# Seven quarter products for the second product of a fused attention and MLP kernel

## The chip, the cores and the metric

One core of one Trainium2 chip. The metric is the device time of one execution in microseconds (us), as the median of several executions. The trace of one execution gives start and duration of every instruction on TensorE (PE; its weight loads PEld), VectorE (DVE), ScalarE (ACT), GpSimd (POOL) and of the DMA queues.

Ratios below are the mean time of one kernel's fast runs over that of the other's of the same rounds on the same chip, so they are not quite the ratio of the medians that are quoted. A run is set aside as slow when it is over 1.5% above the fastest of its kernel.

## The reference

```python
B, H, S, D = 8, 8, 576, 64          # attention: 4 heads with a sliding window of 32,
scores = q @ k.T / sqrt(D)          # 4 heads with every 4th key of the last 128
attn = softmax(where(mask, scores, -1e9)) @ v
x = attn.transpose(0, 2, 1, 3).reshape(4608, 512)
h = x @ w_in                        # 512 -> 2048
g = maximum(h, 0) ** 2
out = g @ w_out                     # 2048 -> 512
```

## The kernel before

The 4608 tokens are cut into nine chunks of 512. For chunk c, the first product gives `ph` (16 tiles of 128 hidden units by 512 tokens), ACT applies relu, DVE squares into `g`; the second product gives four tiles `po` of 128 tokens by 512 outputs. Python generators hand out this work in half-steps (`yield`), and the attention of batch b takes `pump(n)` half-steps of chunk b-1 between its own blocks. So the order on every engine is fixed when the program is built.

```python
def mm1_gen(c, g):
    xs = xT[:, :, c * TOKC : (c + 1) * TOKC]
    for ffc in range(NFF):                                  # 16 steps
        ph = pmool.tile([P, TOKC], FP32, ..., tag="pm")     # 4 PSUM banks in turn
        for dmk in range(NDM):                              # 4 matmuls of 512 columns
            nc.tensor.matmul(ph, wi[...], xs[:, dmk, :], ...)
            if dmk == 1:
                yield
        rt = osb.tile([P, TOKC], FP16, ..., tag="rt")
        nc.scalar.activation(rt, ph[:], ACTF.Relu)
        nc.vector.tensor_mul(g[:, ffc, :], rt, rt)
        yield

def mm2_gen(c, g):
    for t in range(TOKC // P):
        po = pmool.tile([P, DM], FP32, ..., tag="pm")
        for ffc in range(NFF):
            mm2(c, g, po, t, ffc)                           # 16 matmuls of 512 columns
            if ffc % 2 == 1 and ffc < NFF - 1:
                yield
        store(c, t, po)                                     # ACT copy, then a store
        yield

for b in range(2, B):
    pending.append(moe_gen(b - 1))
    ...
    pump(16 if b == 2 else 4)
    attn_scores(b, 4)              # four blocks: matmuls, exp on ACT, mask on DVE
    ...
    attn_values(b, lambda: pump(2 if b == 2 else 3))
    pump(1000)
```

`attn_values` issues the matmuls `pav_0`, `pav_1`, `pav_2` (sliding heads; DVE normalises each into an `x_p` by a reciprocal and a multiplication), the transposes `px_0`, which need the first two `x_p`, then four blocks `paw` with `px_1` and the transposes `py` among them. Score blocks, `pav` and `paw` share two PSUM buffers.

The softmax here doesn't subtract the row's maximum and nothing guards it: scores larger than these inputs give would overflow.

## Time and profile before

| what | value |
|---|---|
| time | 327.25 us, median of 4 (326.17 to 328.54) |
| span of the profiled execution | 327.1 us |
| PE, DVE, ACT busy | 94%, 50%, 51% |
| chunk with attention beside it (chunks 2 to 6) | 32.35 us |
| chunk without (7 and 8) | 27.62 us |
| granted PE clock | 0.984 |

The busy shares are averages over the span. The chain of work that ended last tells which engine sets the pace where: here PE from 80 us to the end. The lines are shown in the prediction.

### The profile page before, as it was taken

To read this page: it belongs to the slowest core of one execution; us is meant where nothing else is said; L and a number is where in the kernel's file an instruction comes from. 1 tells how busy PE (TensorE), PEld (TensorE's weight loads), DVE (VectorE), ACT (ScalarE), POOL (GpSimd) and SP (SyncE) were. 2 spreads that over 40 slices of the span, in tenths; PEclk is the share of its full clock that TensorE was granted. 3 is DMA by queue.
4 is the path that set the end of the run, shared out by engine and by line. 5 is a ranking of instruction groups with operands and counts; after the bars stand their busy time and mean duration, and the time that the engine had idled before them with its cause. 6 is when DMAs were issued, how large, how long until landed. Compare 5 with 4: busy or idle time off the path is not lost.

```text
span 327.1 us, 6310 instructions
## 1 busy us (share of the span) xinstructions
PE 307.9 (94%) x2492; PEld 156.3 (48%) x2492; DVE 162.5 (50%) x348; ACT 168.3 (51%) x300; POOL 81.5 (25%) x139
## 2 busy tenths in 40 slices
PE   5869879996999999999999999999999999999995
PEld 2764344542455455445544554455445544444442
DVE  4584694535662795079408840884098404303500
ACT  2845591264822972397239723972396237415611
POOL 4460660261301800190019001900140010000000
PEclk9999996998999999999999999999999999999999
DMA  8999999989999879589948993899200010021011
GB/s 185 231 194 244 205 183 205 226 171 196 232 205 202 166 171 257 92 178 199 168 142 177 207 197 104 180 207 213 87 34 3 32 66 32 0 95 37 0 64 64
DMA packets 83181, 47.85 MB, mean 146 GB/s; under 512 B 68048, under 2 KB 79056, under 8 KB 82768
## 3 DMA queue, kind: packets, MB, share of 16 engines
q1 hardware_dynamic: 74708, 26.12, 41.5%
q0 software_dynamic: 7072, 19.80, 27.6%
q10 hardware_dynamic: 1372, 1.54, 1.7%
q8 instruction: 19, 0.31, 0.4%
q14 instruction: 10, 0.08, 0.1%
HBM read 39.85 MB, written 16.52 MB: 172 GB/s over the span
## 4 chain that ended last, share of the span: by engine, by line
PE 78%; DMA 12%; ACT 4%; DVE 2%; POOL 1%; issue 1%; SPq 1%; POOLq 0%
PE po L270 35%; PE ph L255 33%; DMA sq<-in_k_dram 6%; DMA QKTx<-dk 3%; DMA dk<-in_k_dram 3%; PE paw L474 2%; PE pav L460 2%; ACT QKTd L143 2%; PE pz L428 1%; PE ps L409 1%; ACT AT L381 1%; PE px L489 1%; PE py L507 1%; DVE AT L382 1%; POOL nq L145 1%
## 5 line engine op out<-in xcount | busy, mean ns | idle before, releaser
L270 PE MATMUL po<-wo,g 128*128 128x512 f16 x576 | 137.7, 384 | 0.0
L255 PE MATMUL ph<-xT,wi 128*128 128x512 f16 x576 | 136.1, 382 | 0.3 <-ACT xT L513 0.3
L266 DVE TENSOR_TENSOR g<-rt 128x512 f16<-128x512 f16 x144 | 76.6, 547 | 105.4 <-ACT rt L265 104.8
L265 ACT ACTIVATE rt<-ph 128x512 f16<-128x512 f32 x144 | 83.8, 604 | 28.5 <-PE ph L255 24.0
L255 PEld LDWEIGHTS <-wi 128*128 128x128 f16 x576 | 52.8, 98 | 58.3 <-issue 1.9
L270 PEld LDWEIGHTS <-g 128*128 128x128 f16 x576 | 53.0, 99 | 55.8 <-issue 2.2
L288 ACT COPY ot<-po 128x512 f32<-128x512 f32 x35 | 20.5, 587 | 72.2 <-PE po L270 72.2
L289 POOL DMA_DIRECT2D out_dram<-ot x28 | 15.5, 553 | 147.9 <-ACT ot L288 147.9
L495 ACT COPY xT<-px 128x576 f16<-128x576 f16 x16 | 10.2, 637 | 25.7 <-PE px L489 25.7
L382 DVE TENSOR_TENSOR AT<-AT,maskp 128x576 f16<-128x576 f16 x32 | 19.6, 636 | 7.6 <-ACT AT L381 7.1
L145 POOL CAST vd<-sd 128x512 f16<-128x512 f32 x32 | 22.9, 754 | 0.0
L443 DVE TENSOR_TENSOR x_d<-paw,rcp_d 72x512 f16<-72x512 f32 x32 | 22.0, 687 | 1.1
L381 ACT ACTIVATE AT<-ps 128x576 f16<-128x576 f32 x32 | 19.2, 657 | 3.7 <-PE ps L409 3.1
L381 ACT ACTIVATE AT<-pz 128x576 f16<-128x576 f32 x32 | 19.2, 669 | 0.3
L161 POOL CAST vp<-sv 128x512 f16<-128x512 f32 x24 | 16.2, 709 | 5.1 <-DMA sv<-in_v_dram 5.1
L442 DVE RECIPROCAL rcp_d<-paw 72x8 f32<-72x8 f32 x32 | 6.5, 202 | 21.9 <-PE paw L474 21.8
L443 DVE TENSOR_TENSOR x_p<-pav,rcp_p 96x512 f16<-96x512 f32 x24 | 16.5, 687 | 0.8
L513 ACT COPY xT<-py 128x576 f16<-128x576 f16 x16 | 10.3, 641 | 11.8 <-PE py L507 11.8
L382 DVE TENSOR_TENSOR AT<-AT,maskd 128x576 f16<-128x576 f16 x32 | 14.9, 495 | 2.4 <-ACT AT L381 2.0
L327 PE MATMUL pj<-zz 128*128 128x128 f16 (+1 forms) x124 | 14.5, 252 | 1.2 <-DVE zz L208 1.2
L474 PEld LDWEIGHTS <-AT 128*128 128x128 f16 x256 | 12.2, 98 | 7.0 <-issue 0.4
L474 PE MATMUL paw<-vd,AT 128*128 128x65 f16 x256 | 13.3, 193 | 0.3 <-DVE rcp_d L442 0.3
(64 smaller groups left out, 144.8 us busy)
## 6 DMA issues: line engine op xcount, KB each, us to landing
out_dram<-ot POOLq DMA_DIRECT2D x28, 256.0 KB, 2.4
sv<-in_v_dram SPq DMA_DIRECT2D x40, 128.0 KB, 7.5
sd<-in_v_dram SPq DMA_DIRECT2D x7, 512.0 KB, 6.3
dk<-in_k_dram POOLq DMA_DIRECT2D x12, 288.0 KB, 6.5
dk<-in_q_dram POOLq DMA_DIRECT2D x12, 288.0 KB, 7.7
wi<-in_moe_w_in_dram POOLq DMA_DIRECT2D x2, 1024.0 KB, 10.6
wo<-in_moe_w_out_dram POOLq DMA_DIRECT2D x4, 512.0 KB, 11.4
sd<-in_v_dram SPq DMA_DIRECT2D x7, 288.0 KB
```

The lines of the kernel that those rows point to most:

```text
L145: eng.tensor_copy(o, i)
L161: nc.gpsimd.tensor_copy(vp[:, m : m + 2, :, 0:D], sv[:, m : m + 2, :, :])
L255: nc.tensor.matmul(ph, wi[:, dmk, ffc * P : ffc * P + P], xs[:, dmk, :], start=(dmk == 0), stop=(dmk == NDM - 1),)
L265: nc.scalar.activation(rt, ph[:], ACTF.Relu)
L266: nc.vector.tensor_mul(g[:, ffc, :], rt, rt)
L270: nc.tensor.matmul(po, g[:, ffc, t * P : (t + 1) * P], wo[:, ffc, :], start=(ffc == 0), stop=(ffc == NFF - 1),)
L288: nc.scalar.copy(ot, po)
L289: (nc.gpsimd if c < B - 1 else nc.sync).dma_start(out=rows, in_=ot)
L381: nc.scalar.activation(AT[:, u, 0:UW], ps[:, :, 0 : UW // 2], ACTF.Exp, scale=scale)
L382: nc.vector.tensor_mul(AT[:, u, 0:UW], AT[:, u, 0:UW], mask)
L443: nc.vector.tensor_tensor(out=x[0:w], in0=pv[:, :, :, 0:D], in1=rcp[0:w].unsqueeze(3).to_broadcast([w, 2, HH, D]), op=ALU.mult,)
L474: nc.tensor.matmul(pav[:, e, h * (D + 2) : h * (D + 2) + D + 1], AT[:, 4 + h, off : off + P], vd[:, t, 2 * a + e, h, 0 : D + 1], start=Tru ...
```

## The change

The idea is Strassen's (in Winograd's form): cut `g` and `w_out` into quarters, and get the product from seven products of quarters instead of eight. It asks for four sums of quarters of `w_out` (made once), four sums of quarters of `g` (for every chunk, on DVE), and for sums of the results, made partly by accumulating in PSUM and partly by DVE. Matmuls have 256 columns instead of 512, and there are 112 instead of 64 of them. Chunk 0 keeps the old product. To make room on DVE, squares now go in pairs of 1024 columns (the last pair singly) and four of the eight pairs move to ACT. To make room in memory, `g` has one buffer instead of two; the trace shows no wait for it at a chunk's start (in chunk 4 ACT's first square starts at 182.28, 0.03 us after the relu that it needs). The attention is spread differently over the half-steps. Core of the diff, cut:

```diff
+    def hidden_sums(g, sm, i0, i1):
+        ...
+        nc.vector.tensor_add(s1, a21, a22)
+        nc.vector.tensor_sub(s2, s1, a11)
+        nc.vector.tensor_sub(s3, a11, a21)
+        nc.vector.tensor_sub(s4, a12, s2)
+
+    BY_ACT = (0, 2, 4, 5)
+    SUMS_AT = {7: (0, 3), 13: (3, 6), 14: (6, 7), 15: (7, 8)}
+
+    def relu_squared(c, ffc, g, ph, rts):
+        ...
+        nc.scalar.activation(rt[:, o, :], ph[:], ACTF.Relu)
+        if i == NK - 1:
+            nc.vector.tensor_mul(g[:, ffc, :], rt[:, o, :], rt[:, o, :])
+        elif o == 1 and i in BY_ACT:
+            nc.scalar.activation(g[:, ffc - 1 : ffc + 1, :], rt, ACTF.Square)
+        elif o == 1:
+            nc.vector.tensor_mul(g[:, ffc - 1 : ffc + 1, :], rt, rt)
...
-            rt = osb.tile([P, TOKC], FP16, name=f"rt{c}_{ffc}", tag="rt")
-            nc.scalar.activation(rt, ph[:], ACTF.Relu)
-            nc.vector.tensor_mul(g[:, ffc, :], rt, rt)
+            relu_squared(c, ffc, g, ph, rts)
+            if sm is not None and ffc in SUMS_AT:
+                hidden_sums(g, sm, *SUMS_AT[ffc])
             yield
...
+        a = bank("poa")
+        yield from product(a, gv[:, :, 0, 0:HT], B11, True)
+        s1 = part("s1")
+        nc.scalar.copy(s1, a)
+        yield
+        b_ = bank("pob")
+        yield from product(b_, sm[:, 1], T[:, 1], True)
+        u2 = part("u2")
+        nc.vector.tensor_add(u2, b_, s1)
+        yield
+        yield from product(a, gv[:, :, 1, 0:HT], B21, False)
+        nc.scalar.copy(otu[:, :, 0:HM], a)
+        ...                             # four more products into b_ and c_, four more additions
...
-        pump(16 if b == 2 else 4)
+        if b == 2:
+            for _ in weight_sums():
+                pump(2)
+            pump(4)
+        else:
+            pump(13)
...
-        attn_values(b, lambda: pump(2 if b == 2 else 3))
+        attn_values(b, lambda: pump(2))
```

In the texts "square 14" is the square of step 14, "sums of pair 6" those of steps 12 and 13, and so on.

More of the change, by code (lines that the diff above doesn't have):

```diff
@@ L57 @@
     stg = ctx.enter_context(tc.tile_pool(name="stg", bufs=1))
-    natp = ctx.enter_context(tc.tile_pool(name="natp", bufs=2))
     xp = ctx.enter_context(tc.tile_pool(name="xp", bufs=4))
-    gp = ctx.enter_context(tc.tile_pool(name="gp", bufs=2))
+    gp = ctx.enter_context(tc.tile_pool(name="gp", bufs=1))
+    tp = ctx.enter_context(tc.tile_pool(name="tp", bufs=1))
     osb = ctx.enter_context(tc.tile_pool(name="osb", bufs=4))
+    otp = ctx.enter_context(tc.tile_pool(name="otp", bufs=3))
     papool = ctx.enter_context(tc.tile_pool(name="papool", bufs=2, space=bass.MemoryType.PSUM))
@@ L83 @@
     sd = stg.tile([P, 2, HH, DIL * D], FP32, name="sd")
-    sq = stg.tile([QB, 2, HH, 6 * D], FP32, name="sq")
+    sq = gp.tile([QB, 2, HH, 6 * D], FP32, name="sq", tag="sm")
+    early = tp.tile([QB, 2, 2, 12 * D * 2], FP16, name="early", tag="T")
+    nq_ = early[:, 0].rearrange("p i (j h d) -> p i j h d", j=6, h=HH)
+    nd_ = early[:, 1].rearrange("p i (g x) -> p i g x", g=2)
     ident = const.tile([P, P], FP16, name="ident")
@@ L113, in load_v, with load_dilated_qk @@
         load_dilated_v(b, nc.sync)
-    def dilated_buffer(b):
-        return natp.tile([QB, 2, 2, 12 * D], FP16, name=f"nd{b}", tag="nd")
-    def load_dilated_qk(b, nd):
+    def load_dilated_qk(b):
         for i, src in ((1, k), (0, q)):
@@ L121, in load_dilated_qk @@
             for e in range(2):
-                nc.gpsimd.dma_start(out=nd[48 * e : 48 * (e + 1), i, :, :], in_=s4[e])
+                nc.gpsimd.dma_start(out=nd_[48 * e : 48 * (e + 1), i, :, :], in_=s4[e])
     def load_w_in():
@@ L147, in cast_sliding_qk @@
     def cast_sliding_qk(b, engs):
-        n = natp.tile([QB, 2, 6, HH, D], FP16, name=f"nq{b}", tag="nq")
         for i in (1, 0):
@@ L153, in cast_sliding_qk @@
                     engs[2 * i + half],
-                    n[:, i, j0 : j0 + 3, :, :],
+                    nq_[:, i, j0 : j0 + 3, :, :],
                     sq[:, i, :, D * j0 : D * (j0 + 3)].rearrange("p h (j d) -> p j h d", d=D),
                 )
-        return n
     def cast_sliding_v(m0=0, m1=NB):
@@ L211 @@
     nc.scalar.activation(warm, warm, ACTF.Exp)
-    nds = {0: dilated_buffer(0)}
-    load_dilated_qk(0, nds[0])
+    load_dilated_qk(0)
     make_identity(nc, ident)
@@ L247, with weight_sums, mm1_gen @@
     )
-    def mm1_gen(c, g):
+    HT = TOKC // 2
+    HM = DM // 2
+    NK = NFF // 2
+    g_of = lambda g: g.rearrange("p (i o) t -> p i o t", o=2)
+    wo_of = wo.rearrange("p (i o) m -> p i o m", o=2)
+    wsum = {}
+    B11, B12 = wo_of[:, :, 0, 0:HM], wo_of[:, :, 0, HM:DM]
+    B21, B22 = wo_of[:, :, 1, 0:HM], wo_of[:, :, 1, HM:DM]
+    def weight_sums():
+        T = wsum["T"] = tp.tile([P, 4, NK, HM], FP16, name="T", tag="T")
+        for i, x, y in (
+            (0, B12, B11),
+            (1, B22, T[:, 0]),
+            (2, B22, B12),
+            (3, B21, T[:, 1]),
+        ):
+            for k0 in range(0, NK, 4):
+                ks = slice(k0, k0 + 4)
+                nc.vector.tensor_sub(T[:, i, ks, :], x[:, ks, :], y[:, ks, :])
+                yield
+    def hidden_sums(g, sm, i0, i1):
+        v = g_of(g)[:, i0:i1]
+        a11, a12 = v[:, :, 0, 0:HT], v[:, :, 1, 0:HT]
+        a21, a22 = v[:, :, 0, HT:TOKC], v[:, :, 1, HT:TOKC]
+        s1, s2, s3, s4 = (sm[:, i, i0:i1, :] for i in range(4))
+        nc.vector.tensor_add(s1, a21, a22)
[5 more added lines that the diff above has]
+    def relu_squared(c, ffc, g, ph, rts):
+        i, o = divmod(ffc, 2)
+        if o == 0:
+            rts[i] = osb.tile([P, 2, TOKC], FP16, name=f"rt{c}_{i}", tag="rt")
+        rt = rts[i]
+        nc.scalar.activation(rt[:, o, :], ph[:], ACTF.Relu)
[5 more added lines that the diff above has]
+            nc.vector.tensor_mul(g[:, ffc - 1 : ffc + 1, :], rt, rt)
+    def mm1_gen(c, g, sm=None):
         xs = xT[:, :, c * TOKC : (c + 1) * TOKC]
+        rts = {}
         for ffc in range(NFF):
@@ L276, in mm2 @@
         )
-    def store(c, t, po):
-        ot = osb.tile([P, DM], FP32, name=f"ot{c}_{t}", tag="ot")
-        rows = out[(c * 4 + t) * P : (c * 4 + t + 1) * P, :]
-        if (c, t) == (NTOKC - 1, 3):
-            h = DM // 2
-            nc.scalar.copy(ot[:, 0:h], po[:, 0:h])
-            nc.sync.dma_start(out=rows[:, 0:h], in_=ot[:, 0:h])
-            nc.vector.tensor_copy(ot[:, h:], po[:, h:])
-            nc.scalar.dma_start(out=rows[:, h:], in_=ot[:, h:])
-            return
-        nc.scalar.copy(ot, po)
-        (nc.gpsimd if c < B - 1 else nc.sync).dma_start(out=rows, in_=ot)
@@ L291, in mm2_gen, with store @@
-    def mm2_gen(c, g):
-        for t in range(TOKC // P):
-            po = pmool.tile([P, DM], FP32, name=f"po{c}_{t}", tag="pm")
-            for ffc in range(NFF):
-                mm2(c, g, po, t, ffc)
-                if ffc % 2 == 1 and ffc < NFF - 1:
-                    yield
-            store(c, t, po)
-            yield
+    def store(c, t, po, ots):
+        if t % 2 == 0:
+            ots[t // 2] = otp.tile([P, 2, DM], FP32, name=f"ot{c}_{t}", tag="ot2")
+        ot = ots[t // 2]
+        nc.scalar.copy(ot[:, t % 2, :], po)
+        if t % 2 == 1:
+            rows = out[(c * 4 + t - 1) * P : (c * 4 + t + 1) * P, :]
+            nc.gpsimd.dma_start(out=rows.rearrange("(t p) m -> p t m", p=P), in_=ot)
@@ new lines, in mm2_strassen_gen, with bank, product, part @@
+    def mm2_strassen_gen(c, g, sm):
+        gv = g_of(g)
+        T = wsum["T"]
+        def bank(name):
+            return pmool.tile([P, 2, HM], FP32, name=f"{name}{c}", tag="pm")
+        def product(acc, lhs, rhs, first):
+            for t in range(2):
+                for k in range(NK):
+                    nc.tensor.matmul(
+                        acc[:, t, :],
+                        lhs[:, k, t * P : (t + 1) * P],
+                        rhs[:, k, :],
+                        start=(first and t == 0 and k == 0),
+                        stop=(k == NK - 1),
+                        skip_group_check=True,
+                    )
+                    if k % 4 == 3 and (t, k) != (1, NK - 1):
+                        yield
+        def part(name):
+            return osb.tile([P, 2, HM], FP32, name=f"{name}{c}", tag="u", bufs=3)
+        def put(half, ot, eng):
+            rows = out[c * TOKC + half * HT : c * TOKC + (half + 1) * HT, :]
+            eng.dma_start(out=rows.rearrange("(t p) m -> p t m", p=P), in_=ot)
+        out_eng = nc.gpsimd if c < B - 1 else nc.sync
+        otu = otp.tile([P, 2, DM], FP32, name=f"otu{c}", tag="ot2")
+        otl = otp.tile([P, 2, DM], FP32, name=f"otl{c}", tag="ot2")
+        a = bank("poa")
+        yield from product(a, gv[:, :, 0, 0:HT], B11, True)
+        s1 = part("s1")
+        nc.scalar.copy(s1, a)
+        yield
+        b_ = bank("pob")
+        yield from product(b_, sm[:, 1], T[:, 1], True)
+        u2 = part("u2")
+        nc.vector.tensor_add(u2, b_, s1)
+        yield
+        yield from product(a, gv[:, :, 1, 0:HT], B21, False)
+        nc.scalar.copy(otu[:, :, 0:HM], a)
+        yield
+        yield from product(b_, sm[:, 2], T[:, 2], False)
+        u3 = part("u3")
+        nc.vector.tensor_add(u3, b_, s1)
+        yield
+        c_ = bank("poc")
+        yield from product(c_, sm[:, 0], T[:, 0], True)
+        nc.vector.tensor_add(otl[:, :, HM:DM], c_, u3)
+        yield
+        yield from product(b_, gv[:, :, 1, HT:TOKC], T[:, 3], False)
+        nc.vector.tensor_add(otl[:, :, 0:HM], b_, s1)
+        put(1, otl, out_eng)
+        yield
+        yield from product(c_, sm[:, 3], B22, False)
+        if c < NTOKC - 1:
+            nc.vector.tensor_add(otu[:, :, HM:DM], c_, u2)
+            put(0, otu, out_eng)
+        else:
+            for t, eng in ((0, nc.sync), (1, nc.scalar)):
+                nc.vector.tensor_add(otu[:, t, HM:DM], c_[:, t, :], u2[:, t, :])
+                r0 = c * TOKC + t * P
+                eng.dma_start(out=out[r0 : r0 + P, :], in_=otu[:, t, :])
+        yield
@@ L305, in mm2_by_rows_gen @@
         ]
+        ots = {}
         for f4 in range(0, NFF, 4):
@@ L312, in mm2_by_rows_gen @@
                 if f4 + 4 == NFF:
-                    store(c, t, po)
+                    store(c, t, po, ots)
                     yield
@@ L320, in moe_gen @@
         g = hidden(c)
-        yield from mm1_gen(c, g)
-        yield from mm2_gen(c, g)
+        sm = gp.tile([P, 4, NK, HT], FP16, name=f"sm{c}", tag="sm")
+        yield from mm1_gen(c, g, sm)
+        yield from mm2_strassen_gen(c, g, sm)
     def idle_matmuls(pj, n, cols):
@@ L347, in pt, with t_sliding @@
         return pmool.tile([P, 1024], FP16, name=name, tag="pm")
-    def t_sliding(b, n, hp, i, wide=False):
+    def t_sliding(b, hp, i, wide=False):
         p_ = pt(f"pt{b}_{hp}_{i}", wide)
@@ L353, in t_sliding @@
                 p_[:, QB * j : QB * (j + 1)],
-                n[:, i, j, 2 * hp : 2 * hp + 2, :],
+                nq_[:, i, j, 2 * hp : 2 * hp + 2, :],
                 ident[0:QB, 0:QB],
@@ L361, in t_sliding, with t_dilated @@
         )
-    def t_dilated(b, n, g, i, wide=False, eng=None):
+    def t_dilated(b, g, i, wide=False, eng=None):
         p_ = pt(f"pd{b}_{g}_{i}", wide)
@@ L367, in t_dilated @@
                 p_[:, QB * j : QB * (j + 1)],
-                n[:, i, g, P * j : P * (j + 1)],
+                nd_[:, i, g, P * j : P * (j + 1)],
                 ident[0:QB, 0:QB],
@@ L516, in x_dilated, with begin @@
         )
-    def begin(b, nq, nd, fill, wide=False):
+    def begin(b, fill, wide=False):
         for hp in range(2):
             for i in (1, 0):
-                t_sliding(b, nq, hp, i, wide)
+                t_sliding(b, hp, i, wide)
                 fill()
@@ L526, in begin @@
             for i in (1, 0):
-                t_dilated(b, nd, g, i, wide, eng=nc.scalar)
+                t_dilated(b, g, i, wide, eng=nc.scalar)
                 fill()
@@ L560, in attn_values @@
         x_dilated(b, 1, zs, wide)
-    nq = cast_sliding_qk(0, (nc.scalar, nc.scalar, nc.vector, nc.gpsimd))
+    cast_sliding_qk(0, (nc.scalar, nc.scalar, nc.vector, nc.gpsimd))
     cast_sliding_v(0, 2)
@@ L574, in idle @@
         idle_matmuls(pj, 5, P)
-    begin(0, nq, nds[0], idle)
-    nds[1] = dilated_buffer(1)
+    begin(0, idle)
     def idle_and_load():
@@ L584, in idle_and_load @@
             nc.vector.memset(sq[:, :, :, 0:1], 0.0)
-            nc.vector.memset(nds[1][:, :, :, 0:1], 0.0)
+            nc.vector.memset(nd_[:, :, :, 0:1], 0.0)
     attn_values(0, idle_and_load)
@@ L589 @@
     load_v(1)
-    load_dilated_qk(1, nds[1])
-    nq = cast_sliding_qk(1, (nc.gpsimd,) * 4)
+    load_dilated_qk(1)
+    cast_sliding_qk(1, (nc.gpsimd,) * 4)
     load_w_out()
@@ L597 @@
     pump(22)
-    begin(1, nq, nds[1], lambda: pump(1))
+    begin(1, lambda: pump(1))
     pump(1000)
@@ L633 @@
             load_v(b + 1)
-        pump(16 if b == 2 else 4)
+        if b == 2:
+            for _ in weight_sums():
+                pump(2)
+            pump(4)
+        else:
+            pump(13)
         attn_scores(b, 4)
```

## The prediction

> **What bounds the kernel now.** I read the busy shares first, then the chain of work that ended last, then the timelines of ScalarE (ACT) and VectorE (DVE).
>
> ```profile
> PE 307.9 (94%) x2492; PEld 156.3 (48%) x2492; DVE 162.5 (50%) x348; ACT 168.3 (51%) x300; POOL 81.5 (25%) x139
> ```
>
> TensorE (PE) is busy 94% of the span. The chain in order of time (start us, us, what) shows that from 79.94 us on it is nearly all PE:
>
> ```profile
> 9.65 0.28 PE pj L327 x5
> ...
> 79.94 0.67 PE ps L409 x12
> ...
> 235.72 2.16 PE ph L255 x10
> ...
> 268.06 13.81 PE ph L255 x64
> 281.88 13.81 PE po L270 x64
> ```
>
> Chunks 2 to 6 start at 106.33, 138.68, 171.02, 203.37 and 235.72, so each takes 32.35 us; chunks 7 and 8, which have no attention beside them, take 27.62 us, half for each product. A 512-column matmul is 13.81/64 = 0.216 us. The change leaves the first product (ph) as it is and thins the second (po).
>
> The shares of 50% hide a crowded stretch. ACT and DVE timelines (start, us, engine, line, operation, count, [idle before]):
>
> ```profile
> 75.20 2.07 ACT L265 ACTIVATE rt<-ph 128x512 f16<-128x512 f32 x4 [1.69 <-DVE g L266]
> ...
> 238.15 1.19 ACT L381 ACTIVATE AT<-ps 128x576 f16<-128x576 f32 x2
> 239.23 1.09 ACT L265 ACTIVATE rt<-ph 128x512 f16<-128x512 f32 x2
> 240.35 1.19 ACT L381 ACTIVATE AT<-ps 128x576 f16<-128x576 f32 x2
> ```
>
> While the four score groups pass, ACT alternates two exps and two relus. Queued relus start every (2.07-0.60)/3 = 0.49 us; two exps hold it 239.23-238.15 = 1.08. So a group costs ACT 1.08+0.98 = 2.06 us of the 2.20 (240.35-238.15) that PE gives it: no room.
>
> ```profile
> 249.23 0.20 DVE L442 RECIPROCAL rcp_p<-pav 96x8 f32<-96x8 f32 x1
> 249.46 0.69 DVE L443 TENSOR_TENSOR x_p<-pav,rcp_p 96x512 f16<-96x512 f32 x1
> 250.07 0.41 DVE L266 TENSOR_TENSOR g<-rt 128x512 f16<-128x512 f16 x1
> 250.40 0.20 DVE L442 RECIPROCAL rcp_p<-pav 96x8 f32<-96x8 f32 x1
> ...
> 270.46 0.42 DVE L266 TENSOR_TENSOR g<-rt 128x512 f16<-128x512 f16 x1 [0.44 <-ACT rt L265]
> ```
>
> Here DVE is queued: a reciprocal and its normalisation take 250.07-249.23 = 0.84 us, a square of 512 takes 0.33 queued and 0.42 to 0.43 alone.
>
> [...]
>
> **The change part by part.** Per chunk, 1 to 8:
>
> 1. PE. 64 matmuls of 512 become 7 x 16 = 112 of 256: 112 x 0.109 = 12.23 us against 13.81. It saves 1.58 us a chunk, 12.6 in all if nothing waits. Weight loads double, but pj shows a load plus 128 columns in 56 ns, so they stay hidden.
>
> 2. ACT. Four of eight square pairs move to it: [...] some 0.95 queued, and 0.14 for the wait on the relu just before: 1.09. Two fewer copies of 0.59.
>
> 3. DVE. From the 0.427, 0.52 ns per element: 0.295 us at 256, 0.56 at 768, 0.695 at 1024; queued 0.085 less, dependent on its predecessor 0.03 more. A group of four sums is then 2.0 us (768) or 0.96 (256); per chunk 2 x 2.0 + 2 x 1.0 = 6.0. Five additions from PSUM at 0.61 queued: 3.1. Squares: three pairs (0.61) and two singles, 2.6 instead of 16 x 0.34 = 5.4. Net about +6.3 us on an engine with room on average.
>
> 4. Once: eight weight sums of 1024, about 5 us of DVE in chunk 1.
>
> Average load says gain. Order says otherwise; I took it from the built kernel's instruction lists. Clock of a chunk (us from its ph0, all from the durations above; attention matmul blocks 0.37 for ps and pz, 0.27 for the others, as the chain has them):
>
> ACT is on time until relu 5 starts at 5.26. Up to relu 13 it then has 8 relus (3.92), 8 exps (4.32), 3 squares (3.27) = 11.5 us, so relu 13 starts at 16.77, ends at 17.37. PE without waits would finish ph13 at 13.56 and that relu could have ended at 14.2: 3.2 us late. PE also idles 0.96 us before pz1, whose two PSUM buffers the previous exps hold.
>
> DVE after relu 13, in its order: square of pair 6 (0.61), sums of pairs 3 to 5 (2.0), square of 14 (0.34), sums of pair 6 (0.96), rcp and x of pav0 (0.84), square of 15 (0.43), sums of pair 7 (1.0), rcp and x of pav1 (0.92 to its end): 7.1 us, so x of pav1 ends at 24.5. PE needs that x for the transposes px0, which lie before product 2. PE's own work from the end of ph13 to px0 is two ph (1.73), three blocks (0.81), product 1 (1.74) = 4.28 us, so unhindered it is there at 17.84. It starts px0 at 24.55: a stall of 6.7 us, 3.5 by DVE's order and 3.2 by ACT's lateness. On the way it waits for square 14 (20.4) and, before pav2, for pav0's x to leave its PSUM buffer (22.2). After px0 I find the additions in time: each has a product of 1.75 us to hide in.
>
> Unhindered chunk: 13.81+12.23+4.45 of attention = 30.5; with 6.7 some 37.2 against 32.35: **+4.8 us, five times: +24**.
>
> Chunks 7 and 8, no attention: the squares of pairs 4 and 5 alone make relu 13 end at 13.41; square 14 then ends at 13.44+2.62+0.43 = 16.5, while PE wants it at 14.57: 1.95 us, and 0.2 more for the last sum in product 2. Minus 1.58: +0.57 each, **+1.1**.
>
> Chunk 1: chunk 0 loses about 1.0 to one square in the stretch from 41 to 50 us where ACT is on the chain, and the loads for batch 2 start after it, so the first scores start at 80.9 instead of 79.94. In front of them now stand four more half-steps of the first product (1.7 us), out of the 3.2 us in which PE waits there. From 80.9 PE has 0.37 + 11 half-steps of 0.43 + 3 x 0.37 + 12.23 + 11 x 0.27 = 21.4 us, and I count 2.5 of waits: 2.2 for square 14, which stands behind the same sums and two masks and ends at 90.45, and 0.3 before pz0. Chunk 2 starts at 104.8 instead of 106.33: **-1.5**.
>
> The end: two PSUM additions of 0.42, then a store, in place of two copies: even. 327.5-1.5+24+1.1 = 351. For PE's clock (below) I add 2: 353.
>
> **The rivals.**
>
> *A. The saving arrives.* PE is the bound, DVE and ACT are half idle, sums hide beside the products: 327.5-12.6, less 1.7 of chunk 1's old wait, plus 1.0 in chunk 0: 314. For it: the 94%. Against it: the in-order list above; 7.1 us of DVE work cannot fit in 4.28 us of PE work whatever the averages.
>
> *B. Only DVE's order counts, ACT keeps up.* Then +3.5-1.58-0.3 (waits of the old chunk) = +1.6, five times, with the others 335. Against it: 11.5 us of ACT work in PE's 8.3.
>
> *C. The clock falls too.* Between 18.5 and 24.5 of my clock PE has 1.4 us of work, 23%. After such stretches this trace shows half clock (window; busy and counts of PE, PEld, DVE, ACT, POOL; clock; DMA):
>
> ```profile
> 48.00:50.00 2.00, 0.86 (x17) 0.61 (x17) 1.63 (x4) 2.00 (x4) 0.00 (x0) 0.66 1.22 197
> 50.00:52.00 2.00, 2.00 (x5) 0.64 (x6) 0.92 (x3) 0.67 (x2) 0.00 (x0) 0.50 1.22 196
> ```
>
> Three microseconds at half clock cost 1.5; in all five chunks +8, about 360.
>
> *D. Smaller matmuls pay the weight load.* At 0.12 to 0.13 us instead of 0.109 the PE saving would vanish, +10 us. Against it: pj.
>
> **Range and chances.** B gives the low side, 335; C the high, 360 to 366. The stall is a sum of some twenty measured terms; 10% on ACT's 11.5 and DVE's 7.1 is 1.9 us a chunk, 9 in all. I take 336 to 366. Faster by 2% (under 320.9) needs the stall to be under about 0.5 us a chunk: 0.06. Within 2% (to 334): 0.08. Slower: 0.86.
>
> **What would show it.** In the changed profile: 256-column matmuls 0.109 us apart where nothing waits (right for part 1; D if 0.12 or more); PE waits on DVE at px, at the first product and at pav2, several us per attention chunk; ACT without idle from relu 6 to relu 15 of each such chunk; chunk starts about 37 us apart, 28.2 for the last two; clock below 0.9 in slices that held a boundary (C). Chunk starts 31 us apart with PE waits near zero would make the prediction wrong, in the reading of the engines' order; 34 us would mean B.

Its sum came to 327.5 - 1.5 + 24 + 1.1 = 351, with 2 for the clock 353. What the traces show for the durations in it:

- PE: 0.216 us for 512 columns (64 in 13.81 us) and 0.056 for 128 (5 `pj` in 0.28) in the kernel before. The 0.109 for 256 lies on the straight line between the two, an estimate; in the changed kernel 16 take 1.75 us, 0.109 each, with as many weight loads as matmuls (2876 and 2876).
- DVE: the 0.427 us is a square of 512 fp16 by itself (0.42 to 0.43 in the lines shown); 512 from PSUM takes 0.69 (`x_p`). The 0.52 ns per element was not shown by the trace before; the changed kernel shows it: in its chunk 4, 256 take 0.28 to 0.29 us, 512 take 0.42, 768 take 0.55 and 1024 take 0.69, so (0.69 - 0.28)/768 = 0.53 ns per element. A sum of 768 that does not need the one before it starts 0.47 us after that one's start (0.08 before its end), one that needs it 0.58 (0.03 after its end).
- ACT: in the kernel before, a relu of 512 takes 0.60 us by itself and 0.49 queued, a cast of 768 takes 0.83. The 1.09 for a square of 1024 (0.95 and 0.14) rests on no square in that trace. In the changed kernel the square takes 1.06, and a relu and the square of it hold ACT 1.59 us (181.65 to 183.24), 1.10 more than a queued relu.
- Order: in chunk 4 of the changed kernel the 19 DVE instructions from 197.22 to 204.24 us start in the order of the program.
- Rival C's "such stretches": in the kernel before PE is busy 0.59 us of the two from 46 to 48 and 0.86 of the next two; the clock is 0.66 from 48 to 50 and 0.50 from 50 to 54.

## The result, and the profile after

The changed kernel took 355.06 us (median of 4, 353.34 to 355.56) against 327.25: ratio 1.0839, 95% interval 1.0784 to 1.0894. It is slower by 8.4%. The prediction was 353, range 336 to 366.

The busy line of the changed kernel's page:

```profile
PE 309.0 (87%) x2876; PEld 199.9 (56%) x2876; DVE 202.8 (57%) x425; ACT 189.4 (54%) x320; POOL 74.2 (21%) x125
```

PE now waits for 13% of the span, while DVE and ACT are still little over half busy. The shares do not show a new bound. The chain that ended last does (start us, us, what), here through chunk 4:

```profile
179.88 6.04 PE ph L307 x28
...
190.91 0.98 PE ph L307 x4
191.90 0.58 ACT rt L293
192.48 1.08 ACT AT L488 x2
194.08 0.87 ACT g L297
195.04 0.58 ACT rt L293
195.62 1.08 ACT AT L488 x2
197.22 0.69 DVE g L299
201.32 0.70 DVE x_p L550
202.16 0.60 PE pav L567 x8
...
213.95 1.75 PE pob L349 x16
215.70 1.75 PE poc L349 x16
217.44 6.04 PE ph L307 x28
```

Chunk 4 takes 217.44 - 179.88 = 37.56 us. In the middle the path leaves PE: it runs over ACT's relus, exps and squares, then over DVE, and comes back to PE at the third block `pav_2` (202.16), which can only start when the first `x_p` is made. Products that wait for nothing run at 1.75/16 = 0.109 us per 256 columns.

The same stretch in PE's timeline, with its idle time in brackets:

```profile
197.68 0.93 PE L349 MATMUL poa<-wo,g 128*128 128x256 f16 x7
200.30 0.28 PE L349 MATMUL poa<-wo,g 128*128 128x256 f16 x1 [1.70 <-DVE g L295]
202.16 0.60 PE L567 MATMUL pav<-vp,AT 128*128 128x65 f16 x8 [1.57 <-DVE x_p L550]
202.57 1.90 PE L349 MATMUL poa<-wo,g 128*128 128x256 f16 x8
```

Seven matmuls of the first product run, the eighth waits 1.70 us for square 14; `pav_2` waits 1.57 us for its PSUM buffer. The last line shows eight matmuls of 256 columns in 1.90 us, against 1.03 for the eight at 206.13: PE's granted clock had fallen (0.50 in 202 to 204 us, 1.00 in 206 to 208). DVE's queue over the same time:

```profile
197.22 0.69 DVE L299 TENSOR_TENSOR g<-rt 128x1024 f16<-128x1024 f16 x1
197.83 0.55 DVE L279 TENSOR_TENSOR sm<-g 128x768 f16<-128x768 f16 x1
...
199.82 0.42 DVE L295 TENSOR_TENSOR g<-rt 128x512 f16<-128x512 f16 x1
...
201.32 0.69 DVE L550 TENSOR_TENSOR x_p<-pav,rcp_p 96x512 f16<-96x512 f32 x1
201.93 0.41 DVE L295 TENSOR_TENSOR g<-rt 128x512 f16<-128x512 f16 x1
...
203.55 0.69 DVE L550 TENSOR_TENSOR x_p<-pav,rcp_p 96x512 f16<-96x512 f32 x1
```

From the square of pair 6 at 197.22 to the end of the second `x_p` at 204.24 DVE is never idle, 7.02 us; its order is that of the program. The relu it waited for is late because of ACT:

```profile
190.94 1.06 ACT L297 ACTIVATE g<-rt 128x1024 f16<-128x1024 f16 x1
...
194.08 1.06 ACT L297 ACTIVATE g<-rt 128x1024 f16<-128x1024 f16 x1
...
196.57 1.64 ACT L293 ACTIVATE rt<-ph 128x512 f16<-128x512 f32 x3
```

The two squares stand among the exps, and the last three relus run as one backlog.

Where the 26.7 us of the two spans (353.8 - 327.1) came from, by starts of chunks in the two chains: chunk 2 starts at 104.72 instead of 106.33 (-1.6); chunks 2 to 6 take 37.56 to 37.60 instead of 32.35 (292.54 - 104.72 against 268.06 - 106.33, together +26.1); chunks 7 and 8 take 28.31 and 28.33 instead of 27.63 (+1.4); from the last matmul to the end it is 4.62 instead of 3.77 us (+0.85).

### The profile page after: what moved, and what is told of

It is laid out like the page before. It is cut to its first block, busy times and chain, and to the rows that moved or that the text cites. A ratio compares the mean times of both kernels' runs of the same rounds, so it can differ in the third digit from the quotient of the medians.

```text
span 353.8 us, 7032 instructions
## 1 busy us (share of the span) xinstructions
PE 309.0 (87%) x2876; PEld 199.9 (56%) x2876; DVE 202.8 (57%) x425; ACT 189.4 (54%) x320; POOL 74.2 (21%) x125
## 4 chain that ended last, share of the span: by engine, by line
PE 64%; ACT 15%; DVE 11%; issue 5%; DMA 2%; POOL 1%; DVEq 0%; POOLq 0%
PE ph L307 22%; PE pob L349 13%; PE poc L349 8%; PE poa L349 7%; ACT rt L293 6%; ACT AT L488 5%; PE po L322 4%; ACT g L297 2%; DMA sq<-in_k_dram 2%; PE paw L581 2%; DVE sm L280 2%; DVE g L299 2%; PE pav L567 1%; PE px L596 1%; DVE sm L279 1%
## 5 line engine op out<-in xcount | busy, mean ns | idle before, releaser
L299 DVE TENSOR_TENSOR g<-rt 128x1024 f16<-128x1024 f16 x27 | 30.8, 1142 | 52.8 <-ACT rt L293 52.6
L349 PEld LDWEIGHTS <-sm 128*128 128x128 f16 x512 | 48.9, 101 | 6.7 <-DVE sm L280 0.6
L349 PE MATMUL poa<-wo,g 128*128 128x256 f16 x256 | 38.8, 297 | 14.2 <-DVE g L295 14.2
L349 PEld LDWEIGHTS <-g 128*128 128x128 f16 x384 | 37.6, 103 | 22.5 <-DVE g L295 16.4
L365 POOL DMA_DIRECT2D out_dram<-otl x6 | 4.5, 757 | 164.6 <-DVE otl L392 164.6
L297 ACT ACTIVATE g<-rt 128x1024 f16<-128x1024 f16 x36 | 38.0, 1057 | 1.1
L349 PE MATMUL pob<-T,sm 128*128 128x256 f16 x256 | 35.6, 285 | 0.0
L373 ACT COPY s<-poa 128x512 f32<-128x512 f32 x8 | 4.7, 585 | 40.2 <-PE poa L349 40.2
L602 ACT COPY xT<-px 128x576 f16<-128x576 f16 x16 | 10.2, 640 | 26.7 <-PE px L596 26.7
L567 PE MATMUL pav<-vp,AT 128*128 128x65 f16 x192 | 11.4, 208 | 12.0 <-DVE x_p L550 7.9
L322 PE MATMUL po<-wo,g 128*128 128x512 f16 x64 | 17.3, 406 | 0.0
```

What stands on the lines that cost most here:

```text
L297: nc.scalar.activation(g[:, ffc - 1 : ffc + 1, :], rt, ACTF.Square)
L299: nc.vector.tensor_mul(g[:, ffc - 1 : ffc + 1, :], rt, rt)
L322: nc.tensor.matmul(po, g[:, ffc, t * P : (t + 1) * P], wo[:, ffc, :], start=(ffc == 0), stop=(ffc == NFF - 1),)
L349: nc.tensor.matmul(acc[:, t, :], lhs[:, k, t * P : (t + 1) * P], rhs[:, k, :], start=(first and t == 0 and k == 0), stop=(k == NK - 1), sk ...
L567: nc.tensor.matmul(pav[:, i, h * (D + 2) : h * (D + 2) + D + 1], AT[:, u, off : off + P], vp[:, m, h, 0 : D + 1], start=True, stop=True,)
L602: nc.scalar.copy(xT[:, 0:2, t0 : t0 + 288], px[:, 0:UW].rearrange("x (c t) -> x c t", c=2),)
```

## The experiments

The theory is the prediction's: engines that work in the order of the program (DVE's queue above, 197.22 to 204.24 us), with a queue on ACT (squares among the exps) and one on DVE (sums in front of squares and of `x_p`) that PE meets at the boundary of the two products. Rivals: DVE's extra work costs its sum wherever it stands; ACT alone is the bound; the fallen clock is most of it; the seven products do not pay on this chip at all.

All timed kernels ran beside the kernel before on the same chip, with 3 rounds.

### Sums of pairs 3 to 5 one step earlier

```diff
-    SUMS_AT = {7: (0, 3), 13: (3, 6), 14: (6, 7), 15: (7, 8)}
+    SUMS_AT = {7: (0, 3), 12: (3, 6), 14: (6, 7), 15: (7, 8)}
```

> Sums of pairs 3 to 5 issued one step earlier (at step 12 instead of 13), nothing else. My theory (DVE's in-order queue holds PE at the boundary): the 2.0 us of these sums leave the queue behind relu 13, but they cannot start before ACT's square of pair 5 ends, so the masks and the square of pair 6 start some 0.65 us later: attention chunks about 36.2 us instead of 37.56, chunks 7 and 8 about 27.3 instead of 28.3, in all 345 us (range 341 to 349). Rival 'ACT alone is the bound': no change, 355. Rival 'the extra DVE work costs its sum wherever it stands': no change, 355.

Measured: fast runs 346.38, 346.59 and 347.84 us, ratio 1.0679 (1.06 to 1.0758). The profiled execution fell in a state with a granted clock of 0.56 and 505.48 us; it is set aside, so no timeline of this kernel is read. The same work at another place in the queue gained 8 us of the 10 expected by the medians, some 5 by the ratios to the kernel before (1.0839 and 1.0679, whose intervals do not overlap). That rules out both rivals that expected no change.

### Squares of pairs 4 and 5 back on DVE

```diff
-    BY_ACT = (0, 2, 4, 5)
+    BY_ACT = (0, 2)
```

> Squares of pairs 4 and 5 go back from ACT to DVE: 2.2 us less of ACT work in front of relu 13, 1.2 us more DVE work. My theory: relu 13 ends about 2.1 us earlier and with it the whole DVE queue behind it; attention chunks about 35.5 us, chunks 7 and 8 about 27.6, chunk 0 and 1 about 1 less: 342 us (range 337 to 347). Rival 'DVE's load is the bound': the 1.2 us added to DVE in each chunk make it slower, 360 or more. Rival 'only the order of DVE counts and ACT's lateness is hidden': 355.

Measured: 343.02 us, ratio 1.0546 (1.0468 to 1.0625), one of four runs slow. DVE got more work and the kernel became faster, by 12 us by the medians and some 9.5 by the ratios, so DVE's load is not what bounds it. Chunks 2 to 5 start at 101.38, 136.99, 173.43, 208.95 and end at 245.28: two take 35.5 to 35.6 us as expected, two take 36.3 to 36.4. The window view tells the two kinds apart (window, busy and counts of PE, PEld, DVE, ACT, POOL, granted clock, DMA). Boundary of chunk 3:

```profile
158.00:160.00 2.00, 1.32 (x15) 1.01 (x13) 1.93 (x7) 0.86 (x2) 0.00 (x0) 0.88 1.10 189
160.00:162.00 2.00, 2.00 (x17) 1.56 (x16) 0.31 (x2) 0.37 (x1) 0.00 (x0) 0.50 1.08 237
162.00:164.00 2.00, 2.00 (x20) 1.60 (x18) 1.35 (x3) 0.40 (x1) 0.00 (x0) 0.77 1.10 216
```

In chunk 3 the clock falls only after PE has waited 0.68 us for the second `x_p` at `px_0`, and the products after that wait run slowly (0.50 in 160 to 162 us). In chunk 2 it falls at 122 us (0.99 in the 2 us before, 0.50 in the 2 us after), earlier by its place in the chunk: PE works slowly up to `px_0` and does not wait there at all. PE waits at `px` in only two chunks of this run. The chunks of the two kinds differ by 0.8 to 0.9 us.

### Attention work six half-steps later

```diff
-            pump(13)
+            pump(19)
```

> All attention work of chunks 2 to 6 moves six half-steps later (scores from half-step 20, values after product 1), so that the normalisations stand behind the hidden sums in PE's order too and PE meets px0 later. My theory: 4.3 us of waits in the chunk instead of 6.7, attention chunks 34.8 us, the last two chunks unchanged at 28.3: 341 us (range 335 to 347). Rival 'the sums cost their time on DVE whatever the order': 355. Rival 'ACT is the bound in the score stretch': the same exps in the same chunk, 353 to 355.

Measured: 340.26 us, ratio 1.0471 (1.0404 to 1.0538). Chunks 3 to 6 take 34.59 us (174.03, 208.62, 243.21, 277.81 are starts), the last two 28.31. The sums and the exps are the same ones: 3.0 us less in each of five chunks by their place alone. Both rivals expected no change. But the edit moves more than the point at which PE meets the sums: four exps now stand behind relu 13, so the square of pair 6 starts 15.6 us after the chunk's start (189.77 - 174.19) instead of 17.3 (197.22 - 179.88). This run does not part ACT's share from DVE's.

### No hidden sums after chunk 1 (wrong result)

```diff
-        sm = gp.tile([P, 4, NK, HT], FP16, name=f"sm{c}", tag="sm")
-        yield from mm1_gen(c, g, sm)
-        yield from mm2_strassen_gen(c, g, sm)
+        if c == 1:
+            wsum["sm"] = gp.tile([P, 4, NK, HT], FP16, name="sm1", tag="sm")
+        yield from mm1_gen(c, g, wsum["sm"] if c == 1 else None)
+        yield from mm2_strassen_gen(c, g, wsum["sm"])
```

> WRONG RESULT ON PURPOSE: the hidden sums are made in chunk 1 only, and chunks 2 to 8 use those of chunk 1; everything else stays. It gives the price of the sums where they stand. My theory: the queue between relu 13 and the x of pav1 shrinks from 7.1 to 3.1 us, so about 4.0 us (plus 0.5 of clock) less in each of five chunks, 2.1 in each of the last two, but 2.7 us of ACT's lateness stay: attention chunks 33 us, last two 26.1, in all 329 (range 325 to 334). Rival 'DVE is the only cause': attention chunks 30.6, in all 316. Rival 'ACT is the only cause': 353.

Measured: 330.00 us, ratio 1.0164 (1.0075 to 1.0253), result wrong as meant. Chunks with attention 33.17 us (171.35 to 204.53), the last two 26.13. The sums cost 37.56 - 33.17 = 4.4 us in a chunk with attention and 2.2 in one without. But even without any sum a chunk with attention takes 0.8 us more than before the change, though PE has 1.58 us less to do: PE still waits 0.33, 0.23 and 0.55 us for exps on ACT and 0.51 for an `x_p` in the chunk, and DVE's queue still starts with the late relus. So neither engine is the only cause.

### The three repairs together

The three edits above that leave the result right, at once.

> The three edits together: sums of pairs 3 to 5 at step 12, squares of pairs 4 and 5 on VectorE, attention work six half-steps later. My theory (in-order queues of ACT and DVE at the boundary): waits fall to about 1 us a chunk (square 14 some 0.5, x of pav0 some 0.5), attention chunks about 31.7 us, last two 26.7, in all 321 (range 315 to 327), so about 2% under the kernel before. Rival 'the extra DVE work makes Strassen a loss here in any order': still 335 or more. Rival 'the three repairs overlap and do not add': 335 to 340.

Measured: 323.65 us, ratio 0.9939 (0.9876 to 1.0002). The repairs nearly add up (8, 12 and 15 us singly, 31 together, by the medians), so the rival "do not add" falls, and so does the one that has Strassen lose in any order. The expected 321 was missed by 2.6 us: chunks 2 to 5 take 32.58 us instead of 31.7, the last two 26.73 as expected. Two waits are left at the boundary:

```profile
151.37 1.16 PE L349 MATMUL poa<-wo,g 128*128 128x256 f16 x9 [0.79 <-DVE g L295]
...
155.36 0.41 PE L567 MATMUL pav<-vp,AT 128*128 128x65 f16 x8 [0.58 <-DVE rcp_p L549]
```

They are 1.37 us instead of the 1.0 that I had counted. The rest of the miss is the unhindered chunk, which I had at 30.5: the reordered version below takes 31.55 with 0.46 us of waits, and the fastest one 31.0 with no wait at the boundary, so 31.0 to 31.1 is nearer.

### The repaired schedule with the old second product

The schedule as in the three repairs, the second product and its stores as before the change, no sums of either kind.

> The schedule of the changed kernel with values later and two square pairs on ACT, but the second product as before the change (64 matmuls of 512 columns), no hidden sums, no weight sums. It tells what of any gain comes from the schedule alone. My theory: PE-bound as the kernel before, attention chunks 32.2 us, last two 27.6, chunk 1's wait for its scores shorter by up to 2 us: 325 (range 321 to 329). Against the three repairs with Strassen the difference is then the saving of 12.6 us less the waits that are left. Rival 'the gain of the repaired version is schedule, not Strassen': this one is as fast as it, near 321 or below.

Measured: 326.88 us, two of four runs slow; the fast runs are 322.94 and 325.13, ratio 0.9961 (0.9877 to 1.0045). Chunks with attention take 32.34 us (100.28 to 132.62), the last two 27.63, as in the kernel before. Its total cannot be told from that of the three repairs. Chunk by chunk the three repairs with Strassen win 0.9 us in each of the last two and lose 0.2 beside attention: there the two waits eat the saving.

### Products reordered

```diff
-            pump(19)
+            pump(21)
...
-        yield from product(a, gv[:, :, 0, 0:HT], B11, True)
+        by_k = [(t, k) for k in range(NK) for t in range(2)]
+        yield from product(a, gv[:, :, 0, 0:HT], B11, True, by_k)
         s1 = part("s1")
         nc.scalar.copy(s1, a)
         yield
+        d_ = bank("pod")
+        yield from product(d_, gv[:, :, 1, 0:HT], B21, True, half(0))
...                                     # then sm1, sm0 and sm2 products with their additions
+        yield from product(d_, gv[:, :, 1, 0:HT], B21, False, half(1))
+        nc.vector.tensor_add(otl[:, :, HM:DM], c_, u3)
+        nc.vector.tensor_add(otu[:, :, 0:HM], d_, s1)
```

on top of the three repairs; the last chunk's upper half is stored in two parts.

> The three edits, attention work two half-steps later still, and the seven products reordered: g11*B11 with k outermost, the first half of g12*B21 in a bank of its own before the first product that needs a sum, its second half where the others wait for VectorE; one more PSUM addition for one ACT copy; last store in two parts. My theory: 3.4 us of PE work stand between the last square and the first use of its sum, so the waits left in the three-edit version go: attention chunks 30.8, last two 26.1, in all 315 (range 311 to 320). Rival: VectorE's queue, with 0.6 us more per chunk, holds PE elsewhere, no better than the three-edit version, 321.

Measured: 316.54 us against 325.57 beside it, ratio 0.974 (0.9683 to 0.9796), result right. It beats both kernels. Chunks with attention 31.55 us, the last two 26.15. Expected was 315, with 30.8 us per chunk with attention. Of the missed 0.75 us per chunk 0.46 lies in two waits; the rest is in no wait that the trace shows, and belongs to the unhindered chunk, counted too short. The waits that are left at a boundary, in its PE timeline:

```profile
151.56 0.28 PE L349 MATMUL pod<-wo,g 128*128 128x256 f16 x1 [0.28 <-DVE g L295]
...
154.28 0.41 PE L580 MATMUL pav<-vp,AT 128*128 128x65 f16 x8 [0.18 <-DVE rcp_p L562]
```

The last two chunks save 27.63 - 26.15 = 1.48 us of the 1.58 that 112 matmuls of 0.109 us can save against 64 of 0.216. Is the gain schedule alone? The repaired schedule with the old product, of the same rounds, has 0.9961 (0.9877 to 1.0045) against 0.974 (0.9683 to 0.9796), and PE's own work with the old product is 27.62 + 4.45 of attention = 32.07 us a chunk, more than the 31.55. The old product with the still later attention was not run.

### The fallen clock: TensorE kept busy in its waits

The changed kernel, with matmuls on zeros in the two long waits (chunks 2 to 6):

```diff
-        yield from product(a, gv[:, :, 0, 0:HT], B11, True)
+        if 1 < c < B - 1:
+            idle_matmuls(a.rearrange("p t m -> p (t m)"), 8, TOKC)
+        for n, _ in enumerate(product(a, gv[:, :, 0, 0:HT], B11, True)):
+            if n == 1 and 1 < c < B - 1:
+                idle_matmuls(bank("warm").rearrange("p t m -> p (t m)"), 6, TOKC)
+            yield
```

> The changed kernel with 8 + 6 matmuls on zeros (512 columns, some 3.0 us in all) put where TensorE idles at the boundary of chunks 2 to 6, before product 1 and before pav2. They should fill the two waits of 1.70 and 1.57 us without moving anything, and hold the clock at full. My reading of the trace: px0 and the first half of product 2 ran at half clock and lost some 0.45 us a chunk, the rest of the half-clock time lay in waits anyway: attention chunks 37.1 instead of 37.56, in all about 353 (2 less than the changed kernel). Rival C of the prediction (half clock costs 1.5 us a chunk): 36.0, in all 347. Rival 'the fill itself delays': longer than 37.6.

Measured: 352.85 us, ratio 1.0871 (1.0805 to 1.0936); the total does not part it from the changed kernel (1.0839), so I read the chunks: 36.95 us each (141.65 to 178.60) instead of 37.56. In the changed kernel's window view the clock had been:

```profile
202.00:204.00 2.00, 1.84 (x15) 1.48 (x16) 1.90 (x8) 0.00 (x0) 0.00 (x0) 0.50 0.89 199
204.00:206.00 2.00, 2.00 (x21) 1.70 (x19) 1.04 (x3) 1.13 (x2) 0.00 (x0) 0.69 1.38 40
```

With the fill it stays at 1.00 through the boundary, and a wait appears that the changed kernel does not have (a window at the boundary of chunk 4, and `px_0` of chunk 3):

```profile
200.00:202.00 2.00, 1.72 (x19) 1.07 (x18) 1.90 (x8) 0.00 (x0) 0.00 (x0) 1.00 0.97 217
```

```profile
165.21 0.34 PE L601 MATMUL px<-ident,x_p 96*128 96x96 f16 x4
166.22 0.26 PE L601 MATMUL px<-ident,x_p 96*128 96x96 f16 x2 [0.68 <-DVE x_p L555]
```

PE, now faster, waits at `px_0` for DVE's second `x_p`, 3.4 us in five chunks. In the changed kernel slow matmuls fill that time. So the clock cost 0.6 us a chunk net, about 3 in all: a follower of the waits, not the main cause. Rival C of the prediction (1.5 us a chunk) is too large for the total, because part of what the slow matmuls lose would be waited for anyway. The clock fell here with waits of 1.70 and 1.57 us that had only 0.3 us of PE work between them, and stayed at 1.00 with 3.0 us of matmuls in them. What decides it, the busy share over some stretch or something else, no run here tests.

### Attention another two half-steps later

```diff
-            pump(21)
+            pump(23)
```

on top of the reordered version.

> The reordered version with the attention work another two half-steps later (scores from half-step 24, values from 40). In the reordered version PE still waits 0.2 us for pav2 and 0.3 us for the last square of product 2's first half per attention chunk; the first of these should go: attention chunks 31.3 instead of 31.55, in all 315 (range 312 to 318). Rival: the values now run past the last product, so the transposes and their copies fall into the next chunk's start, and the time stays at 316.5 or rises.

Measured: 315.64 us (314.62 to 318.97, 5 runs) against 325.52, ratio 0.9685 (0.9646 to 0.9725). Chunks with attention take 31.0 us (198.60 to 229.60). It is the fastest version found; the step from the version before is about its noise in total, but 0.55 us per chunk in the traces. The rival's delay is small: PE waits 0.6 us for `xT` in the whole execution. The profiled execution is its slowest: in chunk 1 PE waits 3.2 us for the transposed q and k, as in the kernel before.

## Why the prediction was right

Its steps, in its own order, against the trace of chunk 4 of the changed kernel (times from the start of the chunk at 179.88):

| step | predicted | measured |
|---|---|---|
| 256-column matmul | 0.109 us | 0.109 |
| relu 13 starts (ACT backlog) | 16.77 | 16.69 |
| DVE queue from pair 6 to second x_p | 7.1 | 7.02 |
| square 14 ends | 20.4 | 20.36 |
| pav2 starts | 22.2 | 22.28 |
| second x_p ends | 24.5 | 24.36 |
| chunk with attention | 37.2 | 37.56 |
| chunks 7 and 8 | 28.2 | 28.31, 28.33 |
| chunk 2 starts | 104.8 | 104.72 |

**The mechanism** was that of the text, and the runs part its two halves: without sums 4.4 us less (I had put 4.0 and 0.5 of clock), without the two squares on ACT about 2.0 less where the clock did not interfere. That both matter excludes rival B, "only DVE's order counts", and rival A by the result itself.

**A sign that did not show.** The prediction named waits of PE for DVE at `px`. In the changed kernel there is none: after `pav_2` the clock is at half (0.50 in 202 to 204 us), the eight matmuls of product 1 take 1.90 us, and PE reaches `px_0` at 204.26, 0.02 us after the second `x_p` ends. The slow work and DVE's queue end together there. Without the slow work the queue does hold PE, as predicted: the filled version waits 0.68 us at `px_0`.

**Mis-sized terms.** (1) The wait before the second group of dilated scores: 0.33 + 0.23 us in the trace instead of 0.96. A wait of 0.55 us for an exp at `pav_0` was not named. That neither shows in the chunk's length, because PE waits for DVE later anyway, is argued. (2) The clock: I added 2 us for it, the filled version shows about 3. (3) "The end: even" was wrong by 0.85 us: the last store is of a 256 KB piece instead of 128 KB. The reordered version stores it in halves and has 3.9 us from last matmul to end, near the 3.77 of before; that the size is the cause is argued from this, not tested alone. (4) The sum for chunk 1 was right by two errors that cancel. The scores began at 78.2 and not at 80.9: the time lost in chunk 0 (its rows start at 50.83 instead of 49.99) was made up before chunk 1 began (69.06 against 69.26 in PE's timelines; in 2 us windows the clock is first below 1.00 from 50 us, in the kernel before from 48), and there was no wait for q and k at all. From there to chunk 2 it took 26.5 us and not 23.9: square 14 was waited for 1.83 us, but matmuls after it ran at a lower clock (0.80, 0.50 and 0.85 in the 2 us windows from 88 to 94 us) and ACT held the score blocks. Why the loads landed earlier in this execution I did not settle; in one run of the fastest version the wait of 3.2 us is there.

**Rival D** (small matmuls pay for their weight loads) fell at once with 0.109 us.

**What the prediction did not say** is that the loss was one of order and not of the method. It named the large waits, and most of their time could be taken away: 355 became 324 by moving work, and 316 by reordering the products.

## What to carry to other kernels

When a change takes work from the bound engine and gives it to engines that are half idle, do not compare busy shares: take the program order on each engine around the point where the engines meet, and add up durations from the trace between the instruction that starts the queue and the one that the bound engine waits for. Here 7.1 us of queue against 4.28 us of PE work, with the 3.2 us by which ACT starts that queue late, told the total within 1% and the loss within 10% (25.5 us of 27.8). If the sum says that it does not fit, the first repair is to move the work or the meeting point, as the experiments did; a method that lost 8.4% in one order gained 3.2% in another.
